# K's first group copied in slot 8, weight steps in other slots, first sums of Q on GpSimd

## The chip, the cores and the metric

One core of a Trainium2 chip runs one program. The metric is the device time of that program in microseconds, the median of several runs. TensorE is called PE here, VectorE DVE, ScalarE ACT, GpSimd POOL; SP is the engine whose queue issues all the transfers of this kernel.

## What is computed

Attention over 2 batches of 8 heads (1152 keys, 64 columns), whose queries are first averaged in pairs (576 queries a head), then two gated layers on the 1152 rows that the heads give together:

```python
q_pool = q.reshape(B, H, S // 2, 2, D).mean(axis=3)
attn = softmax(scale * q_pool @ k.T) @ v              # per head
x = attn_out.transpose(0, 2, 1, 3).reshape(B * S, H * D)
xn = x / rms * rms_g                                   # first layer
x = (g * sigmoid(g) * (xn @ w_val)) @ w_out            # g = xn @ w_gate
out = (sigmoid(x @ w_gate2) * (x @ w_val2)) @ w_out2   # second layer
```

## The kernel before, in words

Every product is made in two parts: an operand is split into a high part `hi` and the remainder `lo`, and PE multiplies hi with hi, hi with lo, and lo with hi. For scores the head's K tile `kk` holds K's hi in one half of the partitions and its lo in the other, so that one matmul makes two of the products; `qq` is laid out to match.

The attention phase is ordered by hand. A head has 18 slots. `at(g, rank, fn)` puts a step into slot g; `run_agenda` (L134) emits slots in order, and the steps of a slot by rank, then by the order in which they were entered. Each engine takes its instructions in that order and waits where data or a buffer is not there.

- **Score units** (`s_unit`, L473, rank 2): 128 queries by 384 keys; three units make a chunk. DVE copies each unit out of PSUM and takes its maximum (`top`, L506, rank 17), ACT makes the exponential of a chunk three slots after its last unit (L519, rank 12). The scores of pair p of heads begin 15 slots ahead of the pair, that is in slot 3 of the second head of the pair before. The first unit reads columns 0 to 384 of the first head's `kk`, the second columns 384 to 768.
- **Transposes of the exponentials** (`t_unit`, L529, rank 3): PE transposes 128 keys of a head in each slot into a PSUM bank `eT`; ACT copies the hi part out in the same slot (L564), DVE the lo part in the next (L565). For the units named in `POOL_UNITS` ACT copies the whole bank to SBUF (`er`, L560), and POOL splits it; in second heads these are the slots 0, 2, 4, 6 and 8. These banks have the tag `t`, of which there are four, shared with the transposes of Q and K and with the first weight step.
- **Preparing a pair** (`prep_pair`, L450, in the first head of the pair before): two groups of Q and three of K are transposed by PE (`q_transposes` L346, `k_transposes` L337), copied by ACT (L458) and split by POOL (L144, L145) into `qa` and into the stores `kh`, `kl`. Then SP copies them, SBUF to SBUF, into the heads' tiles: three copies for Q, the last of which waits for the landing of the others, and four for K (L471): the first head's hi and lo, the second head's hi and lo, 288 KB each. `PREP` and `PREP_MOVES` are the slots of the groups and of the copies, `PREP_SECOND` and `PREP_SECOND_MOVES` those of the first such preparation (pair 1), one slot earlier in the count.
- **The very first pair** (`prep_first`, L361) is prepared at the start: `twice` (L399) sums the neighbouring queries, `part_b` and then `part_a`, one half of the columns on DVE and one on POOL; `head0` and `head1` transpose and split Q and K of the two heads, `SECOND_GROUPS` gives the slots of the second head's groups. `pool_q` (L324) on POOL sums the queries of a later pair.
- **Weight steps during attention** (`w_spread`, L274): five weight tiles are turned from their 64-bit words into fp32 in second heads, in five steps in the slots `W_SLOTS`: ACT scales the high words into a PSUM bank of tag `t` (`w_a1`, L212), DVE makes two passes over it (L230, L234), ACT scales the low words (L219), POOL adds (L240). In first heads, in slot `W_SPLIT`, four of them are split into hi and lo (`w_c`: ACT L254, POOL L255).

After the heads, the two layers run on PE without pause (L733, L836, L865).

Of the kernel before, what the change touches and what calls it, by code (L numbers as in the profile page):

```python
# [16 lines left out]
P = 128  # L17
# [12 lines left out]

EXP_LAG = 3

PREP = (0, 3, 3, 7, 9)
PREP_MOVES = (4, 12)
PREP_SECOND = (1, 5, 6, 11, 11)
PREP_SECOND_MOVES = (11, 13)

PREP_V, POOL_Q, LOAD = 13, 11, 13


FIRST_SUMS, FIRST_Q, SECOND_SUMS, FIRST_V, POOL_Q_SECOND = -1, 3, 4, 7, 11
SECOND_GROUPS = ((5, 3, True, 0), (11, 5, False, 0), (7, 3, True, 1), (11, 3, True, 2), (14, 5, False, 1))
SECOND_DVE = ((False, 1), (True, 0), (True, 2))

W_SLOTS, W_SPLIT = (1, 2, 3, 6, 9), 12
W_WORDS, W_EARLY = 5, 4


# [12 lines left out]
def tile_attention_moe_moe(ctx, tc, q, k, v, w_gate1, w_val1, w_out1, rms_g, w_gate2, w_val2, w_out2, out):  # L63
# [3 lines left out]
    nc = tc.nc  # L67
# [4 lines left out]
    NK = S // P  # L72
# [17 lines left out]
    HP, LP = slice(0, 64), slice(64, 128)  # L90
# [39 lines left out]
    def at(g, rank, fn):  # L130
        count[0] += 1
        agenda.setdefault(g, []).append((rank, count[0], fn))
# [9 lines left out]
    def split(hi, lo, x):  # L142

        nc.gpsimd.tensor_scalar(hi, x, 1.0, 1.0, op0=ALU.mult, op1=ALU.mult)  # L144
        nc.gpsimd.tensor_tensor(lo, x, hi.bitcast(F32), op=ALU.subtract)  # L145
# [203 lines left out]
    def alloc_pair(p):  # L349
        for i in (2 * p, 2 * p + 1):  # L350
            kk[i] = ap.tile([P, NK * P], F32R, tag="kk", bufs=3, name="kk")
            qq[i] = ap.tile([P, 2, SQ], F32R, tag="qq", bufs=3, name="qq")
        return kk[2 * p], kk[2 * p + 1], qq[2 * p], qq[2 * p + 1]

    def move(pairs):
        for dst, src in pairs:
            nc.sync.dma_start(dst.bitcast(F32), src.bitcast(F32))
# [3 lines left out]
    def prep_first():  # L361
# [30 lines left out]
        ka, kb, qa, qb = alloc_pair(0)  # L392

        def twice(j, engines, c):
            if not raw.get(0):
                raw[0] = (None, ap.tile([P, NQC, P], F32, tag="qsum", bufs=1, name="qsum"))
            t = raw[0][1]
            for n, eng in enumerate(engines):
                eng.tensor_tensor(t[:, c, n * D:(n + 1) * D], qr[j][:, c, 0:D], qr[j][:, c, D:2 * D], op=ALU.add)  # L399

        part_a, part_b = slice(0, NCA), slice(NCA, NQC)
# [7 lines left out]
        def head0(g0, is_k, g):  # L409
            t, cs = k_group(0, g) if is_k else q_transposes(0, g)  # L410
            if is_k:
                at(g0, 12, lambda: nc.scalar.activation(ka[HP, cs], t, AF.Copy))
                at(g0, 16, lambda: nc.vector.tensor_tensor(ka[LP, cs], t, ka[HP, cs].bitcast(F32), op=ALU.subtract))
            else:
                at(g0, 12, lambda: nc.scalar.activation(qa[:, 0, cs], t, AF.Copy, scale=QSC))
                at(g0, 16, lambda: nc.vector.scalar_tensor_tensor(qa[:, 1, cs], t, QSC, qa[:, 0, cs].bitcast(F32), op0=ALU.mult, op1=ALU.subtract))

        def head1(g0, is_k, g):
            t, cs = k_group(1, g) if is_k else q_transposes(0, g)
            hi, lo = (kb[HP, cs], kb[LP, cs]) if is_k else (qb[:, 0, cs], qb[:, 1, cs])  # L420
            sc = 1.0 if is_k else QSC
            at(g0, 13, lambda: nc.scalar.activation(hi, t, AF.Copy, scale=sc))
            if (is_k, g) in SECOND_DVE:
                at(g0 + 1, 19, lambda: nc.vector.scalar_tensor_tensor(lo, t, sc, hi.bitcast(F32), op0=ALU.mult, op1=ALU.subtract))
                return
            r = ae.tile([P, 512], F32, tag="kqt", bufs=3, name="kqt")[0:t.shape[0], 0:t.shape[1]]
            at(g0, 13, lambda: nc.scalar.activation(r, t, AF.Copy, scale=sc))
            at(g0 + 1, 21, lambda: nc.gpsimd.tensor_tensor(lo, r, hi.bitcast(F32), op=ALU.subtract))
# [5 lines left out]
        twice(0, (nc.vector, nc.gpsimd), part_b)  # L434
        head0(S00 - 2, False, 1)
        head0(S00 - 2, True, 0)
        at(S00 + FIRST_SUMS, 16, lambda: twice(0, (nc.vector, nc.gpsimd), part_a))
        for g in (1, 2):
            at(S00 - 1, 1, lambda g=g: head0(S00 - 1, True, g))
        at(S00 + FIRST_Q, 1, lambda: head0(S00 + FIRST_Q, False, 0))  # L440
# [5 lines left out]
        at(S00 + SECOND_SUMS, 30, second)  # L446
        for sl, order, is_k, g in SECOND_GROUPS:
            at(S00 + sl, order, lambda sl=S00 + sl, is_k=is_k, g=g: head1(sl, is_k, g))

    def prep_pair(g0, p):  # L450
        ka, kb, qa, qb = alloc_pair(p)
        kst[p] = kh, kl = [ap.tile([P, NK * P], F32R, tag=f"k{s}", bufs=1, name=f"k{s}") for s in "hl"]

        def step(sl, is_k, g):
            t, cs = (k_transposes if is_k else q_transposes)(p, g)
            r = ae.tile([P, 512], F32, tag="kqt", bufs=3, name="kqt")[:, 0:t.shape[1]]
            hi, lo = (kh[:, cs], kl[:, cs]) if is_k else (qa[:, 0, cs], qa[:, 1, cs])
            at(sl, 16, lambda: nc.scalar.activation(r, t, AF.Copy, scale=1.0 if is_k else QSC))  # L458
            at(sl + 1, 21, lambda: split(hi, lo, r))
            if cs.start == 0 and not is_k:  # L460
                at(sl + 1, 22, diagonal)

        def diagonal():
            for h in (HP, LP):
                nc.gpsimd.tensor_copy(qbd[h, :, h], qa[h, :, 0:QH])

        slots, moves = (PREP_SECOND, PREP_SECOND_MOVES) if p == 1 else (PREP, PREP_MOVES)
        for sl, (is_k, g) in zip(slots, ((False, 0), (False, 1), (True, 0), (True, 1), (True, 2))):
            at(g0 + sl, 3, lambda sl=g0 + sl, is_k=is_k, g=g: step(sl, is_k, g))
        at(g0 + moves[0], 45, lambda: move(((qb[LP], qa[LP]), (qb[HP], qa[LP]), (qa[LP], qa[HP]))))  # L470
        at(g0 + moves[1], 45, lambda: move(((ka[HP], kh[HP]), (ka[LP], kl[HP]), (kb[LP], kh[LP]), (kb[HP], kl[LP]))))  # L471

    def s_unit(g, p, k):  # L473

# [220 lines left out]
    END = NHEAD * NJ  # L695
    S0, S00 = -AHEAD, -AHEAD_FIRST
    prep_first()
    at(S0 + FIRST_V, 50, lambda: prep_v(0))
    at(S0 + POOL_Q_SECOND, 50, lambda: pool_q(1))
# [4 lines left out]
    for i in range(NHEAD):  # L704
        p, odd = divmod(i, 2)
        g0 = i * NJ
        for j in range(NJ):
            at(g0 + j, 3, lambda g=g0 + j, i=i, j=j: t_unit(g, i, j))
        if i + 1 < NHEAD:
            at(g0 + PREP_V, 50, lambda i=i: prep_v(i + 1))  # L710
        if not odd and p + 1 < NP:
            at(g0, 0, lambda p=p, g0=g0: prep_pair(g0 + (1 if p else 0), p + 1))
            if p + 2 < NP:
                at(g0 + LOAD, 51, lambda p=p: load_pair(p + 2))
        if odd and p + 2 < NP:
            at(g0 + POOL_Q, 50, lambda p=p: pool_q(p + 2))
        if 0 < p < NP - 1:
            at(g0, 0, lambda g0=g0, odd=odd: w_spread(g0, odd))
# [92 lines left out]
    for layer in range(2):  # L811
# [13 lines left out]
        if layer == 0:  # L825
            alloc_x(1, 0)
            alloc_x(1, 1)
            for dc in range(NDM):
# [3 lines left out]
                for t, fc in [(t, fc) for t in range(TT) for fc in range(NFC)] if last else [(t, fc) for fc in range(NFC) for t in range(TT)]:  # L832
                    w = w_need((0, "o", dc, fc // 4))
                    cs = slice(t * NTT, (t + 1) * NTT)
# [76 lines left out]
```

## Time and profile before

| | us |
|---|---|
| median of 3 runs | 733.63 (732.81 to 734.14) |
| the profiled execution | 734.13 |
| its span, first to last instruction | 732.1 |
| PE busy | 720.0 (98%) |
| DVE busy | 461.5 (63%) |
| ACT busy | 432.9 (59%) |
| POOL busy | 399.0 (54%) |

Attention takes the span up to about 291 us; the layers follow. The page's second part gives PE's granted clock as full in every slice. PE's slices are busy to 9 tenths or more but for the first (7 tenths) and the last (8). DVE and ACT are busy to 7 to 9 tenths as long as attention lasts. A busy span of PE is modelled, and reaches a little past the start of the next matmul; so an idle time in the list of waits is a little less than what was lost.

### The profile page before, as it was taken

To read this page: it belongs to the slowest core of one execution; us is meant where nothing else is said; L and a number is where in the kernel's file an instruction comes from. 1 tells how busy PE (TensorE), PEld (TensorE's weight loads), DVE (VectorE), ACT (ScalarE), POOL (GpSimd) and SP (SyncE) were. 2 spreads that over 40 slices of the span, in tenths; PEclk is the share of its full clock that TensorE was granted. 3 is DMA by queue.
4 is the path that set the end of the run, shared out by engine and by line. 5 is a ranking of instruction groups with operands and counts; after the bars stand their busy time and mean duration, and the time that the engine had idled before them with its cause. 6 is when DMAs were issued, how large, how long until landed. Compare 5 with 4: busy or idle time off the path is not lost.

```text
span 732.1 us, 12456 instructions
## 1 busy us (share of the span) xinstructions
PE 720.0 (98%) x4501; PEld 689.5 (94%) x4501; DVE 461.5 (63%) x1109; ACT 432.9 (59%) x871; POOL 399.0 (54%) x438
## 2 busy tenths in 40 slices
PE   7999999999999999999999999999999999999998
PEld 6899999899999999999999999999999999998886
DVE  7889898889888897778766754322366455553010
ACT  6888888888988884665544545324345445545000
POOL 5677888787877761666434546334145344437100
PEclk9999999999999999999999999999999999999999
DMA  7637382846545001333222324212032123222011
GB/s 194 143 92 175 88 198 60 195 95 166 128 116 130 17 1 30 116 115 119 89 82 87 104 70 144 87 58 88 28 116 87 58 87 115 63 82 87 0 59 71
DMA packets 68860, 70.29 MB, mean 96 GB/s; under 512 B 19328, under 2 KB 60672, under 8 KB 68800
## 3 DMA queue, kind: packets, MB, share of 16 engines
q1 hardware_dynamic: 68800, 69.51, 34.4%
q8 instruction: 35, 0.57, 0.3%
q14 instruction: 25, 0.20, 0.1%
HBM read 52.69 MB, written 2.36 MB: 75 GB/s over the span
## 4 chain that ended last, share of the span: by engine, by line
PE 88%; DVE 3%; POOL 3%; DMA 2%; ACT 1%; issue 1%; SPq 1%; POOLq 0%; DVEq 0%; ACTq 0%
PE acc L733 41%; PE acc L836 10%; PE acc L865 10%; PE s L502 8%; PE o L579 8%; PE eT L552 5%; PE eT L541 3%; DVE e L506 2%; DMA kk<-kl 2%; DVE et L565 1%; POOL kl L145 1%; PE kT L337 1%; ACT e L519 1%; PE oT L612 1%; PE xT L660 1%
## 5 line engine op out<-in xcount | busy, mean ns | idle before, releaser
L733 PE MATMUL acc<-xh,w 128*128 128x384 f32 (+2 forms) x1184 | 295.6, 331 | 0.0
L733 PEld LDWEIGHTS acc<-xh,w 128*128 128x128 f32 x1184 | 211.7, 188 | 0.0
L733 PE MATMUL acc<-xl,w 128*128 128x384 f32 (+2 forms) x592 | 195.5, 330 | 0.0
L255 POOL TENSOR_TENSOR w<-wr,w 128x512 fp32r<-128x512 f32 x68 | 100.2, 1474 | 159.0 <-ACT w L254 158.9
L506 DVE TENSOR_SCALAR_CACHE_REDUCE e<-s 128x384 f32<-128x384 f32 x219 | 119.5, 551 | 26.5 <-PE s L502 24.4
L579 PE MATMUL o<-et,vv 128*128 128x256 f32 (+1 forms) x576 | 125.8, 324 | 0.5 <-DVE e L506 0.3
L240 POOL TENSOR_TENSOR wr<-wsg,wr 128x512 uint32<-128x512 uint32 x72 | 93.9, 1305 | 44.0 <-DVE wsg L234 44.0
L733 PEld LDWEIGHTS acc<-xl,w 128*128 128x128 f32 x592 | 111.2, 188 | 0.0
L502 PE MATMUL s<-kk,qq 128*128 128x384 f32 x396 | 106.8, 355 | 3.1 <-DMA kk<-kl 1.5
L564 ACT ACTIVATE et<-eT 128x512 fp32r<-128x512 f32 (+1 forms) x173 | 83.1, 489 | 25.8 <-PE eT L552 12.6
L565 DVE TENSOR_TENSOR et<-eT,et 128x512 fp32r<-128x512 f32 (+1 forms) x173 | 94.7, 554 | 4.4 <-ACT et L564 3.4
L744 ACT ACTIVATE sg<-acc 128x384 f32<-128x384 f32 (+2 forms) x74 | 35.4, 481 | 96.0 <-PE acc L733 96.0
L519 ACT ACTIVATE e<-e,nb 128x1152 f32<-128x1152 f32 x73 | 91.3, 1251 | 0.4 <-DVE nb L508 0.3
L747 DVE TENSOR_TENSOR sg<-acc,sg 128x384 f32<-128x384 f32 (+2 forms) x74 | 40.5, 547 | 80.5 <-PE acc L733 74.4
L579 PEld LDWEIGHTS o<-et,vv 128*128 128x128 f32 x576 | 82.0, 190 | 2.0 <-DVE et L565 1.4
L212 ACT ACTIVATE wg<-wraw 128x512 f32<-128x512 f32 x72 | 48.2, 670 | 52.9 <-DVE wsg L234 32.2
L234 DVE SCALAR_TENSOR_TENSOR wsg<-wg,wsg 128x512 uint32<-128x512 uint32 x72 | 77.2, 1072 | 2.4
L836 PE MATMUL acc<-hh,w 128*128 128x384 f32 x288 | 73.2, 334 | 0.0
L502 PEld LDWEIGHTS s<-kk,qq 128*128 128x128 f32 x396 | 62.3, 189 | 6.2 <-DMA kk<-kl 1.9
L230 DVE TENSOR_SCALAR wsg<-wg 128x512 uint32<-128x512 uint32 x72 | 42.6, 591 | 35.4 <-POOL wr L240 35.0
L552 PE MATMUL eT<-ident,e 128*128 128x128 f32 x351 | 62.0, 273 | 1.2 <-ACT er L560 1.0
L219 ACT ACTIVATE wr<-wraw 128x512 uint32<-128x512 uint32 x72 | 47.9, 665 | 9.8 <-POOL w L255 8.9
(113 smaller groups left out, 1089.5 us busy)
## 6 DMA issues: line engine op xcount, KB each, us to landing
wraw<-in_moe_w_gate_dram SPq DMA_DIRECT2D x24, 512.0 KB, 3.5
wraw<-in_moe_w_val_dram SPq DMA_DIRECT2D x24, 512.0 KB, 3.5
wraw<-in_moe_w_out_dram SPq DMA_DIRECT2D x24, 512.0 KB, 3.4
qq<-qq SPq DMA_DIRECT2D x21, 288.0 KB, 3.2
vraw<-in_v_dram SPq DMA_DIRECT2D x16, 288.0 KB, 4.4
kraw<-in_k_dram SPq DMA_DIRECT2D x14, 288.0 KB, 5.0
kk<-kh SPq DMA_DIRECT2D x14, 288.0 KB, 4.4
kk<-kl SPq DMA_DIRECT2D x14, 288.0 KB, 5.6
```

The lines of the kernel that those rows point to most:

```text
L234: nc.vector.scalar_tensor_tensor(x["s"], x["g"], 3, x["s"], op0=ALU.logical_shift_left, op1=ALU.bitwise_or)
L240: nc.gpsimd.tensor_tensor(x["r"], x["s"], x["r"], op=ALU.add)
L255: nc.gpsimd.tensor_tensor(t[:, 1], r, t[:, 0].bitcast(F32), op=ALU.subtract)
L502: nc.tensor.matmul(s[:, 0:SU], qs, ks[:, kc], start=(n1 == 0), stop=(n1 == len(products) - 1))
L506: nc.vector.tensor_scalar(e[:, kc], s[:, 0:SU], 1.0, None, op0=ALU.mult, op1=ALU.max, accum_out=m[:, u:u + 1])
L519: at(g + EXP_LAG, 12, lambda: nc.scalar.activation(e, e, AF.Exp, bias=nb, scale=1.0, accum_out=sums[i][:, c:c + 1]))
L552: nc.tensor.transpose(t[:, o:o + P], e[:, ks], ident if c or half else swap_id)
L564: at(g, 12, lambda: nc.scalar.activation(hi, t, AF.Copy))
L565: at(g + 1, 20, lambda: nc.vector.tensor_tensor(lo, t, hi.bitcast(F32), op=ALU.subtract))
L579: nc.tensor.matmul(o[:, 0:n], vv[i][:, kc, :], et[:, k, x * n:(x + 1) * n], start=(done == 0), stop=(done == 2 * NK - 1))
L733: nc.tensor.matmul(acc[:, 0:nt], wt[:, ws, dc * P:(dc + 1) * P], xs[:, dc], start=(dc == 0 and n == 0), stop=(dc == NDM - 1 and n == 2))
L836: nc.tensor.matmul(acc[t][:, 0:NTT], w[:, ws, (fc % 4) * P:(fc % 4 + 1) * P], hs[fc][:, cs], start=(fc == 0 and n == 0), stop=(fc == NFC - ...
```

## The change

`PREP_MOVES` gets four slots instead of two. K's copies to the first head are cut in two: columns 0 to 512 (K's first group) go in slot 8, the rest in slot 12; the copies to the second head stay in slot 12, behind them. That makes six copies for K a pair, instead of four. For pair 1 the copies are in slots 12, 14 and 14 instead of 13, and its groups of Q and K are transposed in slots 3, 6, 7, 11, 12 instead of 1, 5, 6, 11, 11. Two groups of the second head of the first pair go one slot later. The first three weight steps of second heads go one slot later, and the split in first heads goes from slot 12 to slot 16. Both halves of the first `part_a` sums are made by POOL.

```diff
-PREP_MOVES = (4, 12)
-PREP_SECOND = (1, 5, 6, 11, 11)
-PREP_SECOND_MOVES = (11, 13)
+PREP_MOVES = (4, 8, 12, 12)
+PREP_SECOND = (3, 6, 7, 11, 12)
+PREP_SECOND_MOVES = (11, 12, 14, 14)
-SECOND_GROUPS = ((5, 3, True, 0), (11, 5, False, 0), (7, 3, True, 1), (11, 3, True, 2), (14, 5, False, 1))
+SECOND_GROUPS = ((6, 3, True, 0), (11, 5, False, 0), (8, 3, True, 1), (11, 3, True, 2), (14, 5, False, 1))
-W_SLOTS, W_SPLIT = (1, 2, 3, 6, 9), 12
+W_SLOTS, W_SPLIT = (2, 3, 4, 6, 9), 16
-        at(S00 + FIRST_SUMS, 16, lambda: twice(0, (nc.vector, nc.gpsimd), part_a))
+        at(S00 + FIRST_SUMS, 16, lambda: twice(0, (nc.gpsimd, nc.gpsimd), part_a))
-        at(g0 + moves[1], 45, lambda: move(((ka[HP], kh[HP]), (ka[LP], kl[HP]), (kb[LP], kh[LP]), (kb[HP], kl[LP]))))
+        for sl, cs in zip(moves[1:], (slice(0, 4 * P), slice(4 * P, NK * P))):
+            at(g0 + sl, 45, lambda cs=cs: move(((ka[HP, cs], kh[HP, cs]), (ka[LP, cs], kl[HP, cs]))))
+        at(g0 + moves[3], 46, lambda: move(((kb[LP], kh[LP]), (kb[HP], kl[LP]))))
```

## Rows read from the trace of the kernel before

**Rows 1.** PE's waits, 30 to 290 us: who waited, us in total, times, longest.
```profile
PE s L502 <- DMA kk<-kl: 1.5, 2, 0.8
PE eT L552 <- ACT er L560: 1.0, 5, 0.2
```
**Rows 2.** Timeline of PE, start and length in us, around the first such wait.
```profile
132.32 0.55 PE L552 MATMUL eT<-ident,e 128*128 128x128 f32 x3 [0.20 <-ACT er L560]
...
134.40 0.62 PE L502 MATMUL s<-kk,qq 128*128 128x384 f32 x2 [0.82 <-DMA kk<-kl]
134.86 0.49 PE L552 MATMUL eT<-ident,e 128*128 128x128 f32 x3
135.10 0.60 PE L502 MATMUL s<-kk,qq 128*128 128x384 f32 x2
```
**Rows 3.** Timeline of SP's queue before it: Q's three copies, K's second copy.
```profile
121.26 6.72 SPq L357 DMA_DIRECT2D qq<-qq  x3
...
128.71 0.73 SPq L357 DMA_DIRECT2D kk<-kl  x1
```
**Rows 4.** Issue to landing (last column): Q's third copy, K's first and second.
```profile
qq<-qq SPq DMA_DIRECT2D x1, 288.0 KB, 3.0
...
kk<-kh SPq DMA_DIRECT2D x1, 288.0 KB, 4.0
...
kk<-kl SPq DMA_DIRECT2D x1, 288.0 KB, 5.6
```
**Rows 5.** Timeline of PE, the second such wait.
```profile
233.78 0.63 PE L502 MATMUL s<-kk,qq 128*128 128x384 f32 x2 [0.70 <-DMA kk<-kl]
```
**Rows 6.** Timeline of SP's queue before it.
```profile
221.17 5.24 SPq L357 DMA_DIRECT2D qq<-qq  x3
```
**Rows 7.** Issue to landing of K's second copy there.
```profile
kk<-kl SPq DMA_DIRECT2D x1, 288.0 KB, 5.9
```
**Rows 8.** Timeline of PE, slots 2 and 6 of the sixth head.
```profile
99.78 0.55 PE L552 MATMUL eT<-ident,e 128*128 128x128 f32 x3 [0.20 <-ACT er L560]
...
103.50 0.49 PE L552 MATMUL eT<-ident,e 128*128 128x128 f32 x3
```
**Rows 9.** Timeline of ACT, fifth head's weight split to the sixth head's slot 4.
```profile
94.71 0.62 ACT L254 ACTIVATE w<-wr 128x512 fp32r<-128x512 f32 x1
...
101.81 0.44 ACT L564 ACTIVATE et<-eT 128x320 fp32r<-128x320 f32 x1 [0.36 <-PE eT L552]
102.14 1.25 ACT L519 ACTIVATE e<-e,nb 128x1152 f32<-128x1152 f32 x1
103.38 0.43 ACT L560 ACTIVATE er<-eT 128x320 f32<-128x320 f32 x1
```
**Rows 10.** Timeline of PE's weight loads, slot 6 of the twelfth head.
```profile
203.13 0.31 PEld L552 LDWEIGHTS eT<-ident,e 128*128 128x128 f32 x3 [0.20 <-DVE wsg L234]
```
**Rows 11.** Timeline of POOL at the start.
```profile
12.17 0.68 POOL L144 TENSOR_SCALAR vv<-vraw 128x576 fp32r<-128x576 f32 x1 [1.39 <-DMA vraw<-in_v_dram]
...
17.04 0.87 POOL L428 TENSOR_TENSOR qq<-kqt,qq 128x320 fp32r<-128x320 f32 x1
```
**Rows 12.** The line of the first sums: ns min/median/max of one, by engine.
```profile
L399 POOL TENSOR_TENSOR qsum<-first x4: 554/818/878, 3.0 to 9.9; 128x320 f32<-128x320 f32 x2, 128x128 f32<-128x128 f32 x1, 128x192 f32<-128x192 f32 x1
...
L399 DVE TENSOR_TENSOR qsum<-first x2: 293/326/358, 3.0 to 6.3; 128x128 f32<-128x128 f32 x1, 128x192 f32<-128x192 f32 x1
```
**Rows 13.** Timeline of PE at the start.
```profile
17.14 0.55 PE L346 MATMUL qT<-ident,qsum 128*128 128x128 f32 x3 [1.41 <-POOL qsum L324]
...
20.87 0.60 PE L337 MATMUL kT<-ident,kraw 128*128 128x128 f32 x4
21.63 0.62 PE L502 MATMUL s<-kk,qq 128*128 128x384 f32 x2 [0.16 <-DVE e L506]
...
28.11 0.56 PE L579 MATMUL o<-et,vv 128*128 128x320 f32 x2 [0.33 <-DVE e L506]
```

## The prediction

> **What bounds the kernel.** I read the busy shares first: PE is busy in 98% of the span at its full clock, the others in 54 to 63%. So time can come only from PE's own waits, and the next view is the list of them. Ahead of 30 us the start costs a few waits; behind it two kinds matter: two waits of score units for the landing of K's copies, 1.5 us together, and five waits of transposes for ACT's `er`, 1.0 together [rows 1]. The timeline of PE shows what these rows hide. Modelled busy spans overlap the next start (the transposes at 134.86 are 0.49 long, and the unit behind them starts 0.24 later [rows 2]); so each wait costs about 0.15 more than its idle time, about 0.97 and 0.85 for the copies and 0.36 for each of the five banks. That is all the change can win behind 30 us: 1.8 and 1.8. Something over 0.2%, 1.5 us, is about what can be told from no change.
>
> **K's first group sooner.** First place, seventh head into eighth. SP's queue stands behind Q's third copy until 121.26 + 6.72 = 127.98 [rows 3], so slot 8 instead of 12 brings nothing by itself: the first copy of K goes out at 128.0, as before. What it brings is less to move ahead of the first unit. Q's third copy, issued at about 127.5, lands 3.0 later, at 130.5; K's first lands at 128.07 + 4.0 = 132.1, its second at 128.71 + 5.6 = 134.3 [rows 3, 4]. So a whole copy follows another after 1.6 us, once after 2.2. The first part has 512 of 1152 columns: 0.7 each, landing at 131.2 and 131.9. PE would be ready at 134.40 - 0.97 = 133.4, and at 133.05 if the bank wait ahead of it goes too [rows 2]: no wait is left. The second unit needs columns of the second part, 0.70 after the first (134.40 to 135.10). That part takes 0.9 a copy and lands at 133.7 by the common spacing, at 134.4 if it is as late as K's second copy was. So the second unit starts between 133.75 and 134.45 instead of 135.10: a gain of 0.65 to 1.35, bank wait included. I take 1.0, the middle.
>
> Second place, thirteenth head into fourteenth. The queue is free at 221.17 + 5.24 = 226.4 [rows 6]; K's second copy landed 5.9 after its issue and ended the wait at 233.78 [rows 5, 7]. The first part needs only K's first group, so it leaves at 226.4, about 1.4 sooner than the copy that was late, and even 5.9 later is 232.3, before PE's 232.9. The second part carries fewer bytes than the copies did and is needed at 233.6. Gain 0.65 to 0.85; I take 0.75. The other five pairs show no such wait [rows 1] and gain nothing. The two extra issues a pair, some 0.5 us each on SP, stand ahead of the second head's copies and of the loads of V, Q and K, whose users are a head away: nothing, and 0.5 us a pair only if that distance were gone. For pair 1 the copies lose a little of their lead; no wait shows there.
>
> A rule speaks against cutting these copies. The rows show 1.6 us between landings and 3.0 from issue to landing [rows 4], so most of a copy's latency lies beside the copy ahead of it. The Trainium skill (DMA: Bandwidth & Descriptors, "Anatomy of one DMA" and "Rules for kernel authors") gives each transfer some 2.0 us that don't shrink with its size, and advises against two transfers to disjoint partition halves, since they serialize. Were those 2.0 us to add up, a 128 KB part would cost 2.3 by that page and K would land later than now; the rows speak for overlap, and the rival that this makes stands below.
>
> **Weight steps one slot later.** The wait of 0.36 arises so: the first weight step takes a bank of the four in slot 1, and the transposes of slot 2 then get the bank of slot 0, which ACT is still copying [rows 8]. Banks are handed out in the order in which they came free: the transposes of slot 6 got the weight step's bank, and waited for DVE's last pass over it [rows 10]. With the step in slot 2 the same order gives slot 2 an old bank, and the wait there goes. But the step then frees its bank behind slot 4's `er`, so slot 6 gets slot 4's bank instead. In the sixth head that `er` runs at 103.38 for 0.43, behind an exponential of 1.25 which stands behind slot 3's copy, and that copy waits for PE [rows 9]. With PE 0.36 sooner, `er` ends at 103.45; slot 6, now free to start at 103.14, starts at about 103.5, as before [rows 8]. The wait moves from slot 2 to slot 6. I put it at nothing. From below: all five waits go, -1.8. From above: ACT takes the weight split (0.62 [rows 9]) in slot 16 of four first heads, five slots nearer to this chain; its idle time there is 0.36 in the row, and if it can't take the split in, `er` and slot 6 come 0.62 later, +2.5 in four heads. I take nothing because at slot 12 the split merely stood ahead of work that waited for PE. POOL's half (1.3 us) leaves the stretch in which K's last split is due, which delays nobody.
>
> **The start.** The sums of `part_a`: DVE loses 0.36, POOL makes a second sum at up to 0.8 [rows 12]. I put that at nothing, for what decides later is POOL's chain from the landing of V at 12.1: it runs without a gap to 17.04 + 0.87 = 17.91 [rows 11], the lo part of Q that the first score unit of the second head reads. That time stays. With this cover gone it would be worth -0.4 to +0.4. Pair 1's first Q group now stands behind that unit instead of ahead of it: PE had filled the wait of 1.41 with nothing, but did the three transposes (some 0.35) before 17.9 [rows 13]; they now come after. K's first group (four transposes, 0.44) moves behind the unit at 21.63, which waits for DVE either way [rows 13]: +0.44, and the unit itself about 0.1 later. Against it, the last K group goes one slot later, into the wait before 28.11 [rows 13], about -0.35. Sum +0.2, between -0.35 and +0.6. The two groups of the second head one slot later lie ahead of 17.9: nothing.
>
> **Sum.** -1.0 - 0.75 + 0 + 0.2 = -1.55 on the profiled execution's 734.13 (span 732.1 and 2.0 around it): 732.6. That run stands 0.5 over the median of 733.63; on the median it is 732.1.
>
> **Rivals.** (1) The bank waits really go, because PE reaches slot 6 later than I think or ACT sooner: -1.8 more in five heads (the eighth head's is counted above in part, so -1.5): 730.6. Against it: `er` in slot 4 stands behind an exponential [rows 9]. (2) ACT becomes late: the two weight steps that now lie between slot 16 and slot 4 don't fit, slot 6 starts 0.62 later in four heads: -1.55 + 2.5, 734.6. For it: 0.36 of idle time against 0.62 moved in. Against it: ACT had another 0.5 us in hand from slot 12. (3) The copies' gain is smaller and the start's price larger, the change does for K what it says but the second unit waits instead of the first: -0.65 - 0.65 + 0.6, 732.9. (4) Slower: copies cost by number, not by size. If each first-group copy held the queue as long as a whole one, 1.6, the second part would land at 130.5 + 4 x 1.6 = 136.9 in the first place, 1.8 after the start that the second unit had, with the lateness of rows 4 2.4; in the second place, from 229.4 on, at 235.8 to 237, 1.3 to 2.5 after 234.5. Sum about +4 and the start's 0.2: 737.8. It decides from 1.1 to 1.4 us a first-group copy on.
>
> **How the numbers follow.** Forecast 0.43, its own range 731.4 to 732.8; rival 1 0.22; rival 2 0.12; rival 3 0.15; rival 4 0.08. The predicted time is 732.1. The range 730.0 to 734.4 leaves out rival 4 and about half of rival 2. Faster by over 0.2% is below 732.16: rival 1 and a little over half of the forecast, 0.47. Slower is above 735.1: rival 4, 0.08. The rest, 0.45, is the same.
>
> **What will show it.** In PE's list no wait for K's copies at the first units of the eighth and fourteenth heads; perhaps a short one at the second unit of the eighth. Behind slot 2 of second heads no wait for `er`, and one of the same size in slot 6, named ACT `er`; if neither shows, rival 1 holds. The first unit of the second head at 17.97 again, and the wait of 1.41 for POOL's sums gone from the list but replaced by one of that size for POOL's lo part. The prediction would be wrong if PE had work ready at the start that I took for bound by V, or if first-group copies landed over 1.1 us apart.

## The result: 739.3 us, slower than before

| | before | after |
|---|---|---|
| median, us | 733.50 (732.81 to 734.14, 4 runs) | 739.32 (738.15 to 740.92, 4 runs) |
| the profiled execution | 734.13 | 740.92 |
| its span | 732.1 | 738.7 |

The ratio is 1.0081, 95% interval 1.0060 to 1.0102. The forecast was 732.1, its range 730.0 to 734.4. The changed kernel is 5.8 us slower.

In the kernel after, the lines below the edit stand 1 to 3 further down: score units are L505, transposes of exponentials L555, SP's copies L358. PE's waits between 30 and 290 us, the view of [rows 1] (who waited, us in total, times, longest):

```profile
PE s L505 <- DMA kk<-kl: 6.2, 1, 6.2
...
PE eT L555 <- ACT er L563: 0.6, 1, 0.6
```

Both kinds of wait of [rows 1] are gone as they were: the two for K's copies in the eighth and fourteenth heads, and the five of 0.2 for `er` (one of 0.6 is left, in slot 6 of the twelfth head: its transposes start at 210.99, and slot 4's `er`, behind an exponential, ends at 210.52 + 0.42 = 210.94). In their place stands one wait of 6.2 us for K's copies. The timeline of PE says where:

```profile
36.92 0.52 PE L505 MATMUL s<-kk,qq 128*128 128x384 f32 x2
...
43.94 0.98 PE L505 MATMUL s<-kk,qq 128*128 128x384 f32 x2 [6.18 <-DMA kk<-kl]
...
48.88 0.78 PE L505 MATMUL s<-kk,qq 128*128 128x384 f32 x2
```

These are the first, the second and the fourth score unit of pair 1. The first reads K's first group and starts without a wait. The second reads columns of the second part, and waits. It is also nearly twice as long as the unit ahead of it (0.98 against 0.52): the granted clock, the third figure from the right in the stretches below, fell to 0.50, the lower of its two levels (1.2 GHz), and was back at 2.4 GHz before 50 us.

```profile
36.00:44.00 8.00, 1.82 (x15) 1.57 (x13) 2.04 (x7) 3.53 (x8) 2.46 (x4) 0.91 1.02 241
44.00:47.00 3.00, 3.00 (x12) 2.81 (x13) 1.20 (x4) 0.44 (x1) 0.74 (x2) 0.50 0.14 38
...
50.00:55.00 5.00, 5.00 (x37) 4.81 (x37) 3.61 (x14) 4.33 (x8) 3.42 (x4) 1.00 0.00 0
```

(A stretch, its length, the busy time of PE, PE's weight loads, DVE, ACT and POOL, with the number of instructions in brackets, then PE's granted clock, the DMA share, GB/s.) Ahead of the wait, from 37.8 to 43.9, PE had done nothing.

SP's queue of the kernel after tells why the second part was late:

```profile
29.52 0.54 SPq L358 DMA_DIRECT2D kk<-kh  x1
30.16 0.73 SPq L358 DMA_DIRECT2D kk<-kl  x1
33.36 0.33 SPq L319 DMA_DIRECT2D vraw<-in_v_dram  x1
33.74 0.98 SPq L308 DMA_DIRECT2D qraw<-in_q_dram  x2
...
36.20 2.04 SPq L314 DMA_DIRECT2D kraw<-in_k_dram  x2
38.29 0.94 SPq L358 DMA_DIRECT2D kk<-kh  x1
39.28 0.59 SPq L358 DMA_DIRECT2D kk<-kl  x1
```

Between the first part (slot 12) and the rest (slot 14) stand the loads that slot 13 puts on the same queue: V of the next head, then six issues for pair 2's Q and K. The load of V also waits for POOL, whose split of the V before it lasts to 33.33 (31.89 + 1.44), since both use one buffer:

```profile
31.89 1.44 POOL L146 TENSOR_TENSOR vv<-vraw,vv 128x576 fp32r<-128x576 f32 x1
```

In the kernel before, all four K copies of pair 1 were in slot 13 at rank 45, ahead of these loads (ranks 50 and 51). Its queue there:

```profile
29.18 0.46 SPq L357 DMA_DIRECT2D kk<-kh  x1
...
31.20 1.46 SPq L357 DMA_DIRECT2D kk<-kl  x1
32.76 1.29 SPq L318 DMA_DIRECT2D vraw<-in_v_dram  x1
...
37.55 1.94 SPq L313 DMA_DIRECT2D kraw<-in_k_dram  x2
```

The later pairs' slots are counted from one slot further on, so their slot 12 is the head's slot 13, and their copies still stand ahead of the loads. Only pair 1's copies of slot 14 fell behind them.

The chain of waits of the kernel after (start, us, what) goes through exactly this: the last loads' issue, an issue of the rest, and the landing, which the score unit follows at 43.94.

```profile
36.81 1.43 SPq L314
...
38.29 0.94 SPq L358
...
39.28 4.53 DMA kk<-kl
```

**Theories.** (A) The order on SP's queue is the cause: pair 1's rest stands behind slot 13's loads, and the wait and the slower clock behind it are the whole loss. The rest of the change then brings some 3 us. (B) Cutting K into six copies, or preparing pair 1 later, costs by itself, whatever stands ahead. Then I parted the terms of my sum, to see which of them held.

### The profile page after: what moved, and what is told of

It reads as the page before. It is cut to its first block, busy times and chain, and to the rows that moved or that the text cites. A ratio compares the mean times of both kernels' runs of the same rounds, so it can differ in the third digit from the quotient of the medians.

```text
span 738.7 us, 12479 instructions
## 1 busy us (share of the span) xinstructions
PE 722.2 (98%) x4501; PEld 692.8 (94%) x4501; DVE 461.0 (62%) x1108; ACT 432.5 (59%) x871; POOL 399.4 (54%) x439
## 4 chain that ended last, share of the span: by engine, by line
PE 93%; DVE 2%; ACT 1%; DMA 1%; SPq 1%; issue 1%; POOL 0%; ACTq 0%; DVEq 0%
PE acc L736 41%; PE s L505 10%; PE acc L839 10%; PE acc L868 10%; PE o L582 10%; PE eT L555 6%; PE eT L544 4%; PE kT L338 1%; PE qT L347 1%; DVE e L509 1%; DVE et L568 1%; DMA kk<-kl 1%; ACT e L522 1%; PE oT L615 1%; PE xT L663 0%
## 5 line engine op out<-in xcount | busy, mean ns | idle before, releaser
L505 PE MATMUL s<-kk,qq 128*128 128x384 f32 x396 | 108.2, 359 | 9.0 <-DMA kk<-kl 6.2
L505 PEld LDWEIGHTS s<-kk,qq 128*128 128x128 f32 x396 | 63.6, 192 | 11.8 <-issue 6.4
L555 PE MATMUL eT<-ident,e 128*128 128x128 f32 x351 | 61.9, 276 | 1.3 <-ACT er L563 0.6
L544 PE MATMUL eT<-ident,e 128*128 128x128 f32 x288 | 54.0, 275 | 0.0
```

The costliest lines, as they stand in the source:

```text
L505: nc.tensor.matmul(s[:, 0:SU], qs, ks[:, kc], start=(n1 == 0), stop=(n1 == len(products) - 1))
L544: nc.tensor.transpose(t[:, o:o + P], esb[i][c][0][:, ks], ident)
L555: nc.tensor.transpose(t[:, o:o + P], e[:, ks], ident if c or half else swap_id)
```

## Experiments

### The rest of pair 1 ahead of the loads

```diff
-PREP_SECOND_MOVES = (11, 12, 14, 14)
+PREP_SECOND_MOVES = (11, 12, 13, 13)
```

> The changed kernel with one number changed: for pair 1 the rest of K's columns and the second head's copies go in slot 13 instead of 14, so that they stand ahead of the loads of V, Q and K which slot 13 also puts on SP's queue. Theory A (the copies were late because slot 13's loads, one of which waits for POOL, stood ahead of them): the 6.2 us wait of the second score unit of pair 1 at about 37.5 us shrinks to under 0.5, the granted clock between 40 and 60 us is full again instead of 0.83, and the time falls from 739.3 by the 6.4 us lost at that start and by 1 to 4 us of the slower clock behind it: 729.5 to 733. Theory B (cutting K into six copies, or preparing pair 1 one slot later, is at fault by itself, whatever stands ahead): the unit still waits 2 us or more and the time stays above 736.

Measured: 730.64 (730.52 to 731.07, 5 runs), ratio to before 0.9963 (0.9950 to 0.9975). Theory A, B falls: six copies and the later preparation are all there, and the time is 3.1 below before and 8.7 below after. SP's queue and PE of this kernel:

```profile
29.91 0.50 SPq L358 DMA_DIRECT2D kk<-kh  x1
30.50 0.55 SPq L358 DMA_DIRECT2D kk<-kl  x1
...
32.68 1.32 SPq L319 DMA_DIRECT2D vraw<-in_v_dram  x1
```
```profile
36.19 0.52 PE L505 MATMUL s<-kk,qq 128*128 128x384 f32 x2
...
36.79 0.60 PE L505 MATMUL s<-kk,qq 128*128 128x384 f32 x2
...
39.45 0.52 PE L505 MATMUL s<-kk,qq 128*128 128x384 f32 x2
```

The rest leaves 8.4 to 8.8 us sooner, and the second unit follows the first after 0.60. With this the 9.7 us between the two spans (738.7 and 729.0) can be laid out. The first unit of pair 1 stands at 36.92 and 36.19: 0.73 were lost ahead of it. The second stands at 43.94 and 36.79: 7.15, so the wait cost 6.42. From the second unit to the fourth it is 4.94 against 2.66 (39.45 is the fourth), so 2.28 more at the lower clock; the rows that are left up to 50 us make about 0.25. Together 9.7.

### The kernel before with whole copies, one slot later

```diff
-PREP_SECOND_MOVES = (11, 13)
+PREP_SECOND_MOVES = (11, 14)
```

> The kernel before with one number changed: pair 1's four K copies go in slot 14 instead of 13, that is behind slot 13's loads on SP's queue, uncut. Theory A: the loads take about 6.5 us of SP's queue (32.76 to 39.5 in the trace before), so the copies leave from about 39 us on instead of 29.2 and land 4 us later; the first score unit of pair 1, which started at 35.9, waits for them until about 43, some 7 us, and the granted clock falls behind that wait. Time 740 to 745. Theory B: one slot later costs nothing where the copies are whole; 733 to 734.

Measured: 743.33 (742.42 to 743.71, 4 runs), ratio 1.0133 (1.0119 to 1.0147). Nothing else of the change is in it, and it is slower than the changed kernel. Its queue and its PE:

```profile
34.67 2.12 SPq L313 DMA_DIRECT2D kraw<-in_k_dram  x2
36.84 1.25 SPq L357 DMA_DIRECT2D kk<-kh  x1
38.13 0.60 SPq L357 DMA_DIRECT2D kk<-kl  x1
```
```profile
43.76 0.98 PE L502 MATMUL s<-kk,qq 128*128 128x384 f32 x2 [7.69 <-DMA kk<-kl]
```

Here the first unit waits already, for there is no part that went ahead; the clock falls to 0.50 behind it as well. The copies left 2 us sooner than I had expected, since the loads left 0.9 sooner and took SP 5.0 instead of 6.7 (31.88 to 36.84), but the last to be needed landed 5.6 after its issue.

### Which of the loads

The changed kernel, with the load of pair 2 alone two slots later:

```diff
-                at(g0 + LOAD, 51, lambda p=p: load_pair(p + 2))
+                at(g0 + (LOAD if p else 15), 51, lambda p=p: load_pair(p + 2))
```

> The changed kernel as it is, with one load put later: pair 2's Q and K are loaded in slot 15 instead of 13, so that of slot 13's loads only the one of V, which waits for POOL, still stands ahead of the rest of pair 1's K. It parts two causes of the 6.2 us wait. Theory A1 (the time that six load issues take on SP's queue, 33.74 to 38.24 in the trace of the changed kernel): the rest leaves at about 33.8 instead of 38.3 and lands 4.5 later at about 38.3, the second unit waits about 0.8 instead of 6.2, the clock stays full, and the time is 731.5 to 733. Theory A2 (it is V's load, which waits for POOL until 33.36): nearly all of the wait stays, over 4 us, and the time is above 736.

Measured: 731.38 (731.09 to 731.88, 6 runs), ratio 0.9969 (0.9957 to 0.9980). SP and PE:

```profile
32.66 0.33 SPq L319 DMA_DIRECT2D vraw<-in_v_dram  x1
33.05 0.46 SPq L358 DMA_DIRECT2D kk<-kh  x1
```
```profile
37.55 0.59 PE L505 MATMUL s<-kk,qq 128*128 128x384 f32 x2 [0.49 <-DMA kk<-kl]
```

A1: without the six load issues ahead some 0.5 of the wait of 6.2 is left, and the clock stays full. V's load alone costs no more than that half microsecond, since the copies have a lead to lose. Ahead of the six it is not as cheap: in the changed kernel the rest went out 7.4 us after the first part (30.16 + 0.73 = 30.89 to 38.29), of which V's load, with its wait for POOL, held the queue for 2.8 (to 33.36 + 0.33 = 33.69) and the six issues for 4.6. How much of the 6.2 would go if V's load alone were moved was not run.

### The split of K's copies alone

The kernel before, with the cut copies for pairs 2 to 7 and nothing else:

```diff
-PREP_MOVES = (4, 12)
+PREP_MOVES = (4, 8, 12, 12)
...
-        at(g0 + moves[1], 45, lambda: move(((ka[HP], kh[HP]), (ka[LP], kl[HP]), (kb[LP], kh[LP]), (kb[HP], kl[LP]))))
+        if p == 1:
+            at(g0 + moves[1], 45, lambda: move(((ka[HP], kh[HP]), (ka[LP], kl[HP]), (kb[LP], kh[LP]), (kb[HP], kl[LP]))))
+        else:
+            for sl, cs in zip(moves[1:], (slice(0, 4 * P), slice(4 * P, NK * P))):
+                at(g0 + sl, 45, lambda cs=cs: move(((ka[HP, cs], kh[HP, cs]), (ka[LP, cs], kl[HP, cs]))))
+            at(g0 + moves[3], 46, lambda: move(((kb[LP], kh[LP]), (kb[HP], kl[LP]))))
```

> The kernel before, with K's copies to the first head cut in two for pairs 2 to 7 alone (slots 8 and 12, the second head's behind them); pair 1, the weight steps and the start are as before. By the prediction's term: the waits for K's copies at 134.4 and 233.8 us go, 1.0 and 0.75 us, so 731.7. By the rival that copies cost by number: the second units wait instead, about 4 us more than before, 737.5. If two more issues a pair on SP cost 0.5 us each: 6 us, about 738.

Measured: 732.36 (732.27 to 732.73, 11 runs) against 733.74 for before beside it (732.58 to 734.15, 19 runs), ratio 0.9985 (0.9976 to 0.9994). SP in the eighth head's preparation (the first part, then the rest); their time from issue to landing in the last column (128 KB is the first part, 160 KB the rest); and PE:

```profile
127.73 0.55 SPq L357 DMA_DIRECT2D kk<-kh  x1
128.37 0.72 SPq L357 DMA_DIRECT2D kk<-kl  x1
129.19 0.60 SPq L357 DMA_DIRECT2D kk<-kh  x1
129.88 0.55 SPq L357 DMA_DIRECT2D kk<-kl  x1
```
```profile
kk<-kh SPq DMA_DIRECT2D x1, 160.0 KB, 3.1
kk<-kl SPq DMA_DIRECT2D x1, 160.0 KB, 3.5
kk<-kh SPq DMA_DIRECT2D x1, 128.0 KB, 3.2
kk<-kl SPq DMA_DIRECT2D x1, 128.0 KB, 3.2
```
```profile
133.44 0.51 PE L507 MATMUL s<-kk,qq 128*128 128x384 f32 x2
...
134.04 0.60 PE L507 MATMUL s<-kk,qq 128*128 128x384 f32 x2
```

The four parts land at 130.9, 131.6, 132.3 and 133.4, that is 0.6, 0.7 and 1.1 apart, where whole copies were 1.6 to 2.2 apart [rows 3, 4]. Neither unit waits. The second starts at 134.04 instead of 135.10 [rows 2].

### The cut without the sooner slot

The kernel of the last run, with one number changed:

```diff
-PREP_MOVES = (4, 8, 12, 12)
+PREP_MOVES = (4, 12, 12, 12)
```

> The kernel before with K's copies to the first head cut in two for pairs 2 to 7, as in the run of the split alone (732.36), but with both parts in slot 12: the cut without the four slots. By the prediction the cut does the work in the eighth head, since SP's queue stands behind Q's third copy until 128 us whichever slot the first part has, and in the fourteenth head the first part leaves about 1 us later but still lands in time: 732.3 to 732.7. If the sooner slot does the work, the waits at 134.4 or 233.8 us come back in part: 733 to 733.7.

Measured: 732.40 (732.31 to 733.35, 11 runs), ratio 0.9988 (0.9979 to 0.9997), the same as with slot 8. The cut does the work, not the slot. Three of the eleven runs lie between 733.1 and 733.4, and none of the runs with slot 8; whether the sooner slot guards against a late landing in such runs stays open.

### The weight steps alone, and their slots alone

```diff
-W_SLOTS, W_SPLIT = (1, 2, 3, 6, 9), 12
+W_SLOTS, W_SPLIT = (2, 3, 4, 6, 9), 16
```

> The kernel before with the weight steps' slots alone changed (first three steps one slot later, the split in first heads in slot 16). By the prediction's term the five waits of 0.36 us move from slot 2 to slot 6 and nothing is won: 733.5. By the trace of the changed kernel they are there in slot 6, but four of them at about 0.14: a gain of 0.7, 732.8. By the rival that the bank waits go altogether: 731.7. By the rival that ACT becomes late: 736.

With the split left in slot 12:

```diff
-W_SLOTS, W_SPLIT = (1, 2, 3, 6, 9), 12
+W_SLOTS, W_SPLIT = (2, 3, 4, 6, 9), 12
```

> The kernel before with only the first three weight steps of second heads one slot later; the split in first heads stays in slot 12. It parts the gain of the weight steps (731.93 with both moves) into its two halves. If the bank's turn alone is the cause: 732 or a little less, and the stalls in slot 6 are 0.2 as with both moves. If the split's later slot gave part of it, through POOL being free sooner for the last K group of the preparation: 732.5 to 733.

Measured: 731.93 (730.49 to 732.23, 9 runs), ratio 0.9976 (0.9966 to 0.9985), for both moves; 732.20 (731.24 to 733.37, 11 runs), ratio 0.9985 (0.9977 to 0.9994), for the slots alone. My term of nothing was wrong, and the gain is that of the first steps' slots, at least for the most part. ACT, then PE, of the variant with both moves, slots 4 to 6 of the sixth head:

```profile
102.48 0.42 ACT L560 ACTIVATE er<-eT 128x320 f32<-128x320 f32 x1
```
```profile
102.96 0.55 PE L552 MATMUL eT<-ident,e 128*128 128x128 f32 x3
103.26 0.54 PE L579 MATMUL o<-et,vv 128*128 128x320 f32 x2
103.64 0.51 PE L502 MATMUL s<-kk,qq 128*128 128x384 f32 x2
```

Slot 6 starts when slot 4's `er` ends (102.90), as I had said: the wait did move there. But the product behind it, in slot 7, is 0.54 long. In the kernel before it was 0.77, and the unit behind it later by that much:

```profile
103.74 0.77 PE L579 MATMUL o<-et,vv 128*128 128x320 f32 x2
104.35 0.51 PE L502 MATMUL s<-kk,qq 128*128 128x384 f32 x2
```

In the kernel before, the weight load of that product's second half waits for DVE:

```profile
104.09 0.19 PEld L579 LDWEIGHTS o<-et,vv 128*128 128x128 f32 x1 [0.19 <-DVE et L565]
```

DVE shows why, first before, then in this variant: its second pass over the weights (L234) stood ahead of slot 3's lo copy (L565), which the product in slot 7 reads; one slot later it stands behind it.

```profile
102.47 0.69 DVE L234 SCALAR_TENSOR_TENSOR wsg<-wg,wsg 128x512 uint32<-128x512 uint32 x1
...
103.55 0.48 DVE L565 TENSOR_TENSOR et<-eT,et 128x320 fp32r<-128x320 f32 x1
```
```profile
102.70 0.49 DVE L565 TENSOR_TENSOR et<-eT,et 128x320 fp32r<-128x320 f32 x1
103.10 0.68 DVE L234 SCALAR_TENSOR_TENSOR wsg<-wg,wsg 128x512 uint32<-128x512 uint32 x1
```

From slot 6's start to the next unit it is 0.85 before and 0.68 here. What a second head gains in all shows between the Q transposes of two first heads with two second heads between them, at 50.14 and 115.33 in the kernel before, at 50.07 and 114.64 here: 65.19 against 64.57, 0.31 a second head. In the eighth head the gain isn't kept, for there the first unit now waits for K's copy by that much longer (1.2 in the list of waits, where the longest was 0.8). And the other wait for K, at 233.78 [rows 5], doesn't show in this profile: that copy landed 4.2 after its issue, not 5.9 [rows 7]. So part of the 1.8 may belong to a landing that varies, and the steps' own share is, by this profile, four times 0.31, some 1.2. The split's later slot adds nothing that a trace shows: with the slots alone the same stretch is 64.53 (50.20 to 114.73), and the difference of the two times is within their scatter.

### The start put back

The changed kernel with the start and pair 1's preparation as before, so that the cut and the weight steps are left:

```diff
-PREP_SECOND = (3, 6, 7, 11, 12)
-PREP_SECOND_MOVES = (11, 12, 14, 14)
+PREP_SECOND = (1, 5, 6, 11, 11)
+PREP_SECOND_MOVES = (11, 13, 13, 13)
-SECOND_GROUPS = ((6, 3, True, 0), (11, 5, False, 0), (8, 3, True, 1), (11, 3, True, 2), (14, 5, False, 1))
+SECOND_GROUPS = ((5, 3, True, 0), (11, 5, False, 0), (7, 3, True, 1), (11, 3, True, 2), (14, 5, False, 1))
-        at(S00 + FIRST_SUMS, 16, lambda: twice(0, (nc.gpsimd, nc.gpsimd), part_a))
+        at(S00 + FIRST_SUMS, 16, lambda: twice(0, (nc.vector, nc.gpsimd), part_a))
```

> The changed kernel with all that concerns the start and pair 1's preparation put back (groups of the second head and of pair 1 in the old slots, the first sums half on DVE, pair 1's K copies in slot 13, though still cut in two). What is left of the change is the cut of K's copies and the weight steps. Set beside the variant with pair 1's rest in slot 13 (730.64) it prices the start. By the prediction's term the start costs 0.2, between -0.35 and +0.6: 730.0 to 731.0, 730.4 the likeliest. By a rival that the start's new order brings part of that variant's gain: 731.2 to 732.

Measured: 730.68 (730.59 to 731.88, 5 runs), ratio 0.9962 (0.9949 to 0.9974), beside 730.64 with the start as changed. The start's new order is worth nothing that these runs can tell.

### The weight steps later still

Both stand on the kernel of the last run.

```diff
-W_SLOTS, W_SPLIT = (2, 3, 4, 6, 9), 16
+W_SLOTS, W_SPLIT = (3, 4, 5, 7, 9), 16
```

> The variant with the start as before (730.68: cut copies and weight steps in slots 2, 3, 4, 6, 9) with the weight steps in slots 3, 4, 5, 7, 9. There slot 6 of five second heads still starts 0.22 late four times and 0.64 late once, waiting for slot 4's bank, which ACT empties behind an exponential. Theory C (a weight step in a bank moves the wait to the slot whose bank comes next, always at some price): the stalls of slot 6 reappear at slot 7 or 8 with 0.2 or more each, 730.4 to 731.2. Theory D (the price is set only by whether the bank's turn falls on one that ACT empties behind an exponential): in slot 3 the turn falls on a bank of an odd slot, which ACT and DVE empty at once; the five stalls go, 1.3 in sum (4 times 0.2 and 0.55), and the time is 729.4.

```diff
-W_SLOTS, W_SPLIT = (2, 3, 4, 6, 9), 16
+W_SLOTS, W_SPLIT = (5, 6, 7, 9, 12), 16
```

> As the run before it, with the weight steps in slots 5, 6, 7, 9 and 12. Theory C: stalls of 0.2 or more at a slot behind 8, five times; 730.4 to 731.2. Theory D: slot 5 is odd as slot 3, no such stall, 729.4. If ACT is late behind the later steps: above 731.5.

Measured: 730.05 (730.03 to 730.13, 5 runs), ratio 0.9951 (0.9937 to 0.9964), and 729.43 (729.36 to 730.46, 5 runs), ratio 0.9945 (0.9932 to 0.9957). D rather than C: in both the wait for `er` is gone from the list and no other has come; the longest that is left behind 30 us in the second is this, which the kernel before has as well:

```profile
PE s L505 <- DVE e L509: 0.6, 1, 0.6
```

By the medians the second won what D expected, 1.25, and the first half of it, 0.63. By the traces they are closer: the last store leaves SP at 725.66 in the kernel that both stand on, at 724.85 in the first and at 724.61 in the second, 0.81 and 1.05 sooner. What the first lacks besides lies behind the last store, 3.4 us ahead of the end where the other two have 3.0; its cause is open. The second beats both kernels: 0.55% below the kernel before (733.99 beside it, 9 runs), and 9.9 us below the changed one.

## Why the prediction was wrong

**The step that failed.** "For pair 1 the copies lose a little of their lead; no wait shows there." I put that at nothing. It cost +8.7 us (739.32 against 730.64), and neither my sum nor a rival nor the range has it. I had counted the instructions of the moved step and the slots it moved by, but not what it was moved past: between slot 13's rank 45 and slot 14 stand slot 13's own loads on the same queue. I looked for a wait at pair 1, found none, and took that for room. The sum could have been made from rows of before. There the loads take SP from 32.76 to 37.55 + 1.94 = 39.49, 6.7 us. A copy behind them leaves at 39.5, the second of the two some 0.6 later, and lands 4.0 or more after that [rows 4], at 44.1. The second unit of pair 1 wants it at about 36.5 to 37. That is a wait of some 7 us; 6.42 were measured.

**The clock.** I let no wait cost more than itself. The 6.42 cost another 2.5 at the lower clock.

**K's first group sooner** (-1.75): right in mechanism, and near in size. Measured -1.4 by the medians, -1.1 (-1.8 to -0.4) by the ratio. In the eighth head the landings came within 0.3 of those worked out for the first part and 0.3 sooner than the common spacing gave for the rest, and the second unit started 1.06 sooner where I had taken 1.0 with the bank wait gone as well, which this variant still has. That slot 8 brings nothing by itself also held. The two waits were mis-sized all the same: I took what one execution lost for what every execution loses. Three other profiles have the copies of these pairs whole, and each shows one of the two waits: those with the weight steps' slots moved that of the eighth head (1.16 and 1.12), the one with pair 1's whole copies late that of the fourteenth (0.60). The kernel before spreads over 1.6 us, the variant with the cut over 0.5. That the spread comes from these landings is argued, not shown. One reading was wrong too: in the fourteenth head the late copy [rows 7] was the second of the two, which the cut lets out some 0.8 sooner, not 1.4, and 5.9 later would have been 232.9, the moment when PE wants it. It landed 4.4 after its issue in this variant, so nothing came of the slip. The rule of the Trainium skill that I set against the rows (DMA: Bandwidth & Descriptors, "Rules for kernel authors": two transfers to disjoint partition halves aren't worth it) does not speak of this cut: K's hi and lo went to the two halves as two copies before and after, and what was cut is the columns. The fixed 2.0 us stand in the Trainium skill (DMA: Bandwidth & Descriptors, "Anatomy of one DMA") for transfers that GpSimd issues, and SP issues these. The parts landed 0.6 to 1.1 apart, so nothing like 2.0 added up, and the time fell.

**The weight steps** (0): right in place, wrong in size. The wait did move from slot 2 to slot 6, but not whole. In the sixth head 0.42 went at slot 2 (from one score unit to the next 98.73 to 100.87 before, 98.31 to 100.03 in the variant) and 0.30 came at slot 6 (102.28 to 102.96 from the product ahead of it, which takes 0.38 before). And I had taken "starts at about 103.5, as before" for the end of the matter: I had costed the first step, which takes the bank, and not the passes of DVE, which move with it. They had cost PE another 0.17 behind slot 6, and that went. Together that is some 0.3, the 0.31 a head. No list of waits shows the 0.17, for PE counts as busy there; the timeline of PE of before has the product at 103.74 with 0.77 beside its usual 0.54, one row behind those that I read. With the first step in slot 5 the stretch of two second heads is 64.30 (50.19 to 114.49) against 65.19 before, 0.44 a head, so slot 2 still left 0.13. Rival 1 came nearest in time for this term, and by luck: the wait of slot 6 that it denies is there. Rival 2, ACT late, is not seen.

**The start** (+0.2, between -0.35 and +0.6): 0.0. As foreseen, the wait of 1.41 [rows 13] is replaced by one of that kind for POOL's lo part, 1.7 long in the profile of after. The unit that waited came at 17.45, not at 17.97, since V landed sooner: its first split began at 11.67, not at 12.17. The chain of POOL that I had counted on held, with 5.8 from that split to the unit in both, and in the variant with pair 1's rest in slot 13 as well (12.05 to 17.83).

**The rival that ended slower** (copies cost by number, 737.8) came near to the time by another cause. Its own condition, first-group copies over 1.1 us apart, is not met: 0.6.

So my sum without the failing step, with the terms as measured, is -1.4 - 1.8 + 0 = -3.2, and 730.64 is -3.1. So close a fit is in part luck: a landing that varies may stand in both terms, and by the profiles, with 0.31 in five heads once the copies come in time, the sum is -1.4 - 1.55 = -2.95.

## What to carry to other kernels

When a step with transfers moves to another slot, list every issue of that queue between its old and its new place, with what each of them waits for, before you say that it "loses a little lead"; a distance in slots says nothing of a queue that is served in order. That no wait shows at a place tells that there is some room, not how much: find the moment when the data is used and count back. A step that holds a buffer out of a shared set costs by whose buffer the next user then gets, so try it behind each of its neighbours.

## What the runs showed that I had not expected

PE's granted clock fell to 0.50 behind the waits of 6.18 and 7.69 us, and was full again 3 to 6 us later. At a shorter wait two executions differed. In the profile of the changed kernel, behind a wait of 1.7 us for POOL's lo part, it fell as well:

```profile
18.00:21.00 3.00, 3.00 (x18) 2.87 (x16) 2.61 (x9) 2.72 (x5) 1.64 (x4) 0.62 0.15 58
```

In the variant with the rest of pair 1 ahead of the loads, whose instructions are the same up to there, the wait was 1.9 and the clock stayed:

```profile
18.00:21.00 3.00, 3.00 (x24) 2.87 (x24) 2.63 (x9) 2.47 (x5) 1.34 (x2) 1.00 0.37 127
```

At the end of that wait the changed kernel was 0.38 ahead of the variant (17.45 against 17.83), at pair 1's first unit 0.73 behind, so 1.11 were lost between; the clock missing in this one stretch is 0.38 of 3.00 us, 1.14. That the clock is the whole of it was not shown. What decides between the two stays open; the mean granted clock of the four runs of the changed kernel, 0.993 to 0.997, goes with their times (740.92 at 0.993, 738.15 at 0.997).
